# Row length of five of the zero fills in a DMA-bound attention backward kernel: fills 0 and 1 to 56 KB rows, fills 16, 22 and 23 to 28 KB rows

## The chip, the cores and the metric

The kernel runs on one core of a Trainium2 chip. The metric is the device time of one execution in microseconds (us). A profiled execution has a page and a trace; the page's span is about 1.8 us shorter than the time. Each run is labelled fast or slow: slow is a run more than 1.5% above the fastest of the same kernel.

## The reference, cut to what matters

The reference computes a decode step (sliding-window attention over a cache, a small MLP as a gate) and all its gradients. What matters here is the size of the outputs:

```
k_cache, v_cache: (B=2, Hkv=8, Sk=32768, Dh=128) bf16;  window W = 4096
k = k_cache[:, :, Sk - W:, :]      # only the last 4096 of 32768 rows are used
...
return out, d_x, d_k_cache, d_v_cache, d_wq, d_wo, d_w1, d_b1, d_w2, d_b2
```

The gradients of the two caches (out_2, out_3) have the caches' full shape, and their first 28,672 rows per head are zero. So 32 parts (2 caches x 2 batches x 8 heads) of 28,672 x 128 x 2 B = 7.34 MB each must be written with zeros: 235 of the 327 MB that the kernel moves. Each part is one "fill".

## The kernel before

Fills 0 to 30 are issued from GpSimd (POOL), all read the same tile of zero bytes `zt` and cast it to the output's type on the way. The last, 31, is issued from the SP queue at the end.

```python
ZG = 112
zt = const.tile([P, ZG * DH], mybir.dt.uint8, name="zt")
nc.vector.memset(zt[:].bitcast(F32), 0.0)

def zf(o, q, r0, nent, rows, rep=1):        # nent partitions, each writes rep runs of `rows` cache rows
    ...
    w = rows * DH
    if w > ZG * DH:                         # 224 rows: written as f32, so that zt is long enough
        v = v.bitcast(F32); w //= 2
    v = v.rearrange("(r p g) d -> p r (g d)", p=nent, g=rows)
    ...                                     # st: a step of 4 partitions for small pieces, else 1
    zs = zt[0:nent * st:st, 0:w].unsqueeze(1).to_broadcast([nent, rep, w])
    sw_fill.append(nc.gpsimd.dma_start(out=v, in_=zs))

zlong = (3, 5, 7, 11, 12, 16, 17, 18, 19, 22, 23, 24, 25, 26, 27, 28, 29, 30)
zshort = {2: (...), 4: (...), 6: (...), 8: (...), 10: (...), 13: (...), 15: (...), 20: (...)}   # patched fills
for qi in range(ZQ - 1):
    r = 0
    whole = (P, ZR // P, 1) if qi in zlong else (P, ZG, ZR // (P * ZG))   # 56 KB rows, or 28 KB rows twice
    for n, rows, rep in zshort.get(qi, (whole,)):
        r = zf(*zparts[qi], r, n, rows, rep)
```

A "long" fill writes one row of 57,344 B per partition, a "short" one two rows of 28,672 B.

Beside the fills runs the compute chain. It starts with small loads on ACT's queue and large ones on SP's:

```python
dma_store.dma_start(out=b1_bf[:], in_=B_b1.rearrange("(p j) -> p j", j=FK))   # 28 B per partition
dma_store.dma_start(out=b2_bf[:], in_=B_b2.rearrange("(p k) -> p k", k=DK))   # 8 B per partition
dma_load.dma_start(out=w1, ...); dma_load.dma_start(out=w2, ...)
dma_load.dma_start(out=wo[:], ...); dma_load.dma_start(out=wq[:], ...)
vnat = load(A_v_cache, 0, "v")
```

Then come four rounds. Each works on a V tile and a K tile of 4.19 MB, overwrites them with their gradients, stores them (ACT's queue) and loads the next ones into the same buffers. In the last round PE also transposes `oT_all` (line 473), the first step of the output. At the end:

```python
last = nc.sync.dma_start(out=out_6.rearrange("(p k) f -> p k f", k=DK), in_=dw1_st)   # "the dw store"
...                                                     # v, zs: fill 31, 14,336 B rows
with tc.issue_after(last.ins):
    fin = nc.sync.dma_start(out=v, in_=zs)              # also waits for fill 29 (sw_fill[-2])
```

So the dw store marks the end of compute, and fill 31 starts when both the dw store is issued and fill 29 has landed.

## Time and profile before

| | before |
|---|---|
| time, median (4 runs, all fast) | 766.55 us (766.38 to 766.66) |
| DMA rate over the span | 427 GB/s, 326.73 MB |
| PE / DVE / ACT busy | 50% / 36% / 28% |
| first K load issued | 107.3 us |
| dw store issued, fill 31 issued | 701.0 us, 719.1 us |

The first fence is from the page of the kernel before: busy time of each engine (us, share, instructions), the DMA engines' busy tenths and GB/s in 40 equal slices, and the packets, MB and share of each queue. Queue 0 is the fills, 1 is SP's, 10 is ACT's.

```profile
PE 385.0 (50%) x4109; PEld 232.4 (30%) x4118; DVE 275.8 (36%) x483; ACT 214.6 (28%) x313; POOL 35.0 (5%) x67
...
DMA  9999999999999999999999999999999999999998
GB/s 362 426 428 428 436 419 440 435 429 427 426 428 432 430 448 430 413 428 430 438 426 440 430 427 438 425 426 434 437 433 433 433 418 440 431 425 440 430 416 377
...
q0 software_dynamic: 8000, 227.55, 70.4%
q1 hardware_dynamic: 2696, 56.63, 19.2%
q10 hardware_dynamic: 1736, 41.95, 13.6%
```

No compute engine is busy much over half the time, and the DMA engines are at least 90% busy in every slice but the last. The rate is 427 GB/s over the span, and only the first and the last slice fall well below that.

Two lines from the timeline of SP's queue (start us, duration us, what), then the line of SP's waits (total, times, longest) that says what fill 31 waited for:

```profile
107.30 0.54 SPq L217 DMA_DIRECT2D nat<-in_A_k_cache_dram  x1
...
700.97 0.33 SPq L637 DMA_DIRECT2D out_dram<-dw  x1
719.05 0.39 SPq L642 DMA_DIRECT2D out_dram<-zt  x1
```

```profile
SPq L642 <- DMA out_dram<-zt: 17.7, 1, 17.7
```

Fill 31 waited 17.7 us for a fill after compute had ended: compute was not the last to come.

POOL's timeline: after eight issues it waits for fill 0 to land before it may issue more (the bracket is the idle time and what ended it).

```profile
4.92 5.22 POOL L101 DMA_DIRECT2D out_dram<-zt  x8 [3.26 <-DVE zt L81]
43.62 0.60 POOL L101 DMA_DIRECT2D out_dram<-zt  x1 [33.48 <-DMA out_dram<-zt]
```

PE's timeline at line 473. PE stops in mid-group for 7.78 us; "issue" means that the profile shows nothing that it waited for.

```profile
559.96 3.63 PE L408 MATMUL ps<-t,nat 128*128 128x16 bf16 x128
563.52 0.90 PE L473 MATMUL tp<-ident_bf,oT_all 128*2 128x128 bf16 x7
572.20 1.01 PE L473 MATMUL tp<-ident_bf,oT_all 128*2 128x128 bf16 x8 [7.78 <-issue]
```

### The profile page before, as it was taken

The numbers are of one execution on the slowest core, as the hardware profiler recorded it, in microseconds if no ns is written. First come the engines' busy times: TensorE is split into PE (matmuls) and PEld (weight loads), VectorE is DVE, ScalarE is ACT, GpSimd is POOL, SyncE is SP. The second block draws the span as 40 slices with busy tenths as digits, with TensorE's granted clock in tenths as the row PEclk, the third lists the DMA queues.
The fourth block names the chain that finished last, engine by engine and source line by source line (L and its number), as shares of the span: only waits on it lengthen the run. The fifth ranks groups of instructions, "written<-read, shape, count | busy, mean of one in ns | idle before, by whom it ended". The sixth has DMA issues, their size and how long they took to land.

```text
span 764.6 us, 9390 instructions
## 1 busy us (share of the span) xinstructions
PE 385.0 (50%) x4109; PEld 232.4 (30%) x4118; DVE 275.8 (36%) x483; ACT 214.6 (28%) x313; POOL 35.0 (5%) x67
## 2 busy tenths in 40 slices
PE   0166773747503757850665672017539667585000
PEld 0153352533102535420343430015435433231000
DVE  3034252455401447540434652004443526664000
ACT  0034441245500144540113552002323335143000
POOL 3000010010000000000000000000000000000000
PEclk9998898857755886875579686558957657555555
DMA  9999999999999999999999999999999999999998
GB/s 362 426 428 428 436 419 440 435 429 427 426 428 432 430 448 430 413 428 430 438 426 440 430 427 438 425 426 434 437 433 433 433 418 440 431 425 440 430 416 377
DMA packets 12473, 326.73 MB, mean 427 GB/s; under 512 B 2898, under 2 KB 2906, under 8 KB 2934
## 3 DMA queue, kind: packets, MB, share of 16 engines
q0 software_dynamic: 8000, 227.55, 70.4%
q1 hardware_dynamic: 2696, 56.63, 19.2%
q10 hardware_dynamic: 1736, 41.95, 13.6%
q8 instruction: 32, 0.52, 0.3%
q14 instruction: 9, 0.07, 0.0%
HBM read 45.62 MB, written 280.50 MB: 427 GB/s over the span
## 4 chain that ended last, share of the span: by engine, by line
DMA 33%; PE 32%; DVE 11%; ACT 9%; issue 6%; ACTq 0%; DVEq 0%; SPq 0%
DMA out_dram<-nat 14%; DMA nat<-in_A_k_cache_dram 11%; PE ov L419 7%; PE tp L385 5%; DMA b_bf<-in_B_b_dram 4%; DMA nat<-in_A_v_cache_dram 4%; ACT p_bf L453 2%; PE ps L408 2%; ACT nat L157 2%; ACT tring L157 2%; PE s_ps L392 2%; DVE nat L159 2%; PE wps L586 2%; DVE tring L159 2%; PE dops L312 1%
## 5 line engine op out<-in xcount | busy, mean ns | idle before, releaser
L385 PE MATMUL tp<-pperm,nat 128*128 128x128 bf16 x1024 | 91.2, 241 | 142.5 <-DMA nat<-in_A_v_cache_dram 119.3
L159 DVE COPY tring<-tp 128x1024 bf16<-128x1024 bf16 (+1 forms) x98 | 66.0, 689 | 177.4 <-PE tp L385 168.4
L385 PEld LDWEIGHTS <-nat 128*128 128x128 bf16 x1024 | 67.7, 108 | 162.1 <-DMA nat<-in_A_v_cache_dram 121.2
L157 ACT CAST nat<-ov 128x512 bf16<-128x512 f32 x160 | 87.5, 590 | 64.6 <-PE ov L419 42.5
L157 ACT COPY tring<-tp 128x1024 bf16<-128x1024 bf16 (+1 forms) x34 | 34.4, 1011 | 226.1 <-PE tp L385 200.5
L159 DVE CAST nat<-ov 128x512 bf16<-128x512 f32 x96 | 65.6, 690 | 54.7 <-PE ov L419 52.2
L101 POOL DMA_DIRECT2D out_dram<-zt x58 | 33.4, 580 | 529.2 <-DMA out_dram<-zt 525.9
L419 PE MATMUL ov<-bd,ds_bf 128*128 128x512 bf16 x124 | 48.0, 460 | 6.5 <-DVE nat L159 3.7
L419 PE MATMUL ov<-bd,p_bf 128*128 128x512 bf16 x123 | 47.8, 456 | 5.4 <-DVE nat L159 1.4
L408 PE MATMUL ps<-t,nat 128*128 128x16 bf16 x1024 | 28.8, 173 | 14.0 <-issue 7.2
L408 PEld LDWEIGHTS <-nat 128*128 128x128 bf16 x1024 | 28.7, 103 | 16.9 <-issue 11.7
L392 PEld LDWEIGHTS <-zz 128*32 128x32 bf16 x512 | 17.7, 96 | 36.9 <-issue 27.1
L392 PE MATMUL s_ps<-tring,zz 128*32 128x256 bf16 x256 | 19.7, 294 | 14.3 <-ACT tring L157 6.8
L159 DVE CAST wq<-wps 128x512 bf16<-128x512 f32 x16 | 11.0, 691 | 41.3 <-PE wps L579 41.1
L400 PE MATMUL tp<-ident_bf,p_bf 128*128 128x128 bf16 x64 | 7.5, 312 | 34.9 <-ACT p_bf L453 34.9
L392 PE MATMUL dp_ps<-tring,zz 128*32 128x256 bf16 x256 | 20.2, 322 | 7.7 <-ACT tring L157 4.9
L453 ACT ACTIVATE p_bf<-e_sb,rl 32x512 bf16<-32x512 f32 x16 | 22.8, 1424 | 3.4 <-DVE rl L450 3.2
L157 ACT CAST wq<-wps 128x512 bf16<-128x512 f32 x16 | 9.3, 587 | 51.0 <-PE wps L579 51.0
L466 DVE SCALAR_TENSOR_TENSOR ds_bf<-dp_ps,delta,p_bf 32x512 bf16<-32x512 f32 x16 | 21.7, 1357 | 0.3
L419 PEld LDWEIGHTS <-ds_bf 128*128 128x128 bf16 x128 | 13.0, 108 | 20.6 <-issue 18.3
L419 PEld LDWEIGHTS <-p_bf 128*128 128x128 bf16 x128 | 12.9, 110 | 19.9 <-issue 17.3
L400 PEld LDWEIGHTS <-p_bf 128*128 128x128 bf16 x64 | 6.5, 146 | 35.9 <-ACT p_bf L453 35.9
(195 smaller groups left out, 442.4 us busy)
## 6 DMA issues: line engine op xcount, KB each, us to landing
out_dram<-zt POOLq DMA_DIRECT2D x23, 7168.0 KB, 103.3
out_dram<-nat ACTq DMA_DIRECT2D x8, 4096.0 KB, 41.1
out_dram<-zt POOLq DMA_DIRECT2D x7, 3584.0 KB, 64.6
nat<-in_A_v_cache_dram SPq DMA_DIRECT2D x4, 4096.0 KB, 31.5
nat<-in_A_k_cache_dram SPq DMA_DIRECT2D x4, 4096.0 KB, 26.3
out_dram<-zt SPq DMA_DIRECT2D x1, 7168.0 KB, 44.6
out_dram<-zt POOLq DMA_DIRECT2D x2, 3488.0 KB, 67.7
out_dram<-zt POOLq DMA_DIRECT2D x1, 6120.0 KB, 85.8
```

The source lines that it names most:

```text
L101: sw_fill.append(nc.gpsimd.dma_start(out=v, in_=zs))
L157: nc.scalar.copy(out=out_ap, in_=in_ap)
L159: nc.vector.tensor_copy(out=out_ap, in_=in_ap)
L312: nc.tensor.matmul(dops[0:B, :, :], lhsT=dsT_bf[:, dk, :], rhs=woT[:, :, dk, :], start=(dk == 0), stop=(dk == DK - 1))
L385: nc.tensor.transpose(tp[:, j, :], nat[:, g * CC + half * CH + j, :], pperm[:].rearrange("p b k -> p (b k)"))
L392: nc.tensor.matmul(out_ps[pr * RB:(pr + 1) * RB, half * CH * PB:(half + 1) * CH * PB], lhsT=zbuf[:, pr, o:o + RB], rhs=tT[:, :, pr, :], st ...
L400: nc.tensor.transpose(tp[:, cc, :], src[:, half * CH + cc].rearrange("r k b -> r (k b)"), ident_bf[:, :])
L408: nc.tensor.matmul(ps[:], lhsT=nat[:, g * CC + half * CH + cc, :], rhs=cols[half][:, cc, :, g, :], start=(half == 0 and g == 0 and cc == 0 ...
L419: nc.tensor.matmul(ov[:], lhsT=src[:, cc].rearrange("r k b -> r (k b)"), rhs=bd[:, gh * 4:(gh + 1) * 4, :], start=True, stop=True)
L453: nc.scalar.activation(out=p_bf[rb, :, :, pr], in_=e_sb[rb], func=ACT.Copy, scale=rl[rb, 0:1])
L466: nc.vector.scalar_tensor_tensor(out=ds_bf[rb, :, :, pr], in0=dp_c[rb], scalar=delta[rb, 0:1], in1=p_bf[rb, :, :, pr], op0=ALU.subtract, o ...
L586: nc.tensor.matmul(wps[:], lhsT=o_rows[:, j:N:NJ], rhs=ds_rows[:, :], start=True, stop=True)
```

## The change

```diff
-    zlong = (3, 5, 7, 11, 12, 16, 17, 18, 19, 22, 23, 24, 25, 26, 27, 28, 29, 30)
+    zlong = (0, 1, 3, 5, 7, 11, 12, 17, 18, 19, 24, 25, 26, 27, 28, 29, 30)
```

That is all of it. Bytes, order and dependencies stay. The intent can only be in how the fills share the 16 DMA engines with loads and stores: longer rows give the first two fills a larger share, shorter rows give three later fills a smaller one.

## The prediction

> **What bounds the kernel.** The DMA engines. The page's DMA row reads 9 (90% or more busy) in 39 of 40 slices, at 427 GB/s over the span; PE is busy 50%, DVE 36%, ACT 28%. The packet records, in 8 us windows, show 424 to 434 GB/s from 16 to 760 us. 326.7 MB must move, and the change moves the same bytes. The Trainium skill ("DMA: Bandwidth & Descriptors", Specifications) gives 435 GB/s as the fabric ceiling; the trace sits 1 to 2% below it.
>
> **What the change does.** A fill of 7.34 MB goes out as 256 packets of 28,672 B or 128 of 57,344 B. The packet records give 1079 and 2155 ns: per byte 0.1% apart. Windows of fills alone run at 429 to 432 GB/s with long rows, 426 to 431 with short ones. Two fills become long, three short: 128 more packets in queue 0 (8128), same bytes, at most an estimated 0.3 us. POOL's order stays.
>
> **What moves: shares.** The same page (Queues, rings and completion order) says an engine round-robins between queues packet by packet. The trace agrees: against loads of 32,768 B packets, 28 KB fills take about 205 of 430 GB/s (24 to 72 us), 57 KB fills about 271 (464 to 480 us). So:
> - Fills 0 and 1 run at 9.5 to 78 us, beside the loads of w1, w2, wo, wq and the first V, and will take 60 to 80% of the engines instead of half. Fill 0 should land near 34 us (now 43.6, by POOL's waits), fill 1 near 61 (now 77.8), the V tile about 10 us later.
> - The critical chain starts with the bias load b2, 8 B rows, landed at 32.9 us after 8 rounds of about 2.31 us (1079 + 1231). A round with a long packet costs 3.39 us, so I estimate b2 at 40 to 43 us and compute 8 to 10 us later: first K load issued near 116 us instead of 107.3.
> - Fills 16, 22 and 23 run at about 405 to 420 and 545 to 580 us, where the fill queue is alone. Short rows help nobody there, unless the later schedule brings a transfer.
>
> **How much is critical.** Almost nothing: the delay is on the compute chain, which is not the bound. The SP waits show that the last fill, issued on SP at 719.1 us, waited 17.7 us for a fill, not for the store of dw issued at 701.0; compute may be 18 us later before that wait changes. Even then POOL's last fill (done about 745 us) keeps the engines full some 20 us more. Part of the delay should vanish, because a late transfer meets fills that have advanced.
>
> **Prediction:** 766.4 us, 80% range 764.6 to 768.6. Faster by over 2%: 0.01; within 2%: 0.97; slower by over 2%: 0.02.
>
> **What would show it right.** Queue 0 with 8128 packets and 227.55 MB; span mean 426 to 428 GB/s; the first wait in the chain (b_bf) 39 to 41 us instead of 30.9; POOL's first wait for a fill about 10 us shorter; first K load at 113 to 119 us; dw store 0 to 12 us later; last SP fill within 3 us of 719, still released by a fill.
>
> **What would make it wrong.** (a) Delays that add up: transfers that shift from short onto long fills cost about 8 us per 4 MB, and with some 38 us in sum the fills run dry before compute ends. (b) Long packets starving the w1 and w2 loads more than the shares say. (c) Long packets leaving the 16 engines more skewed at the end.

One remark for reading it: its times from packet records were taken on a clock that runs 1.2 us ahead of the page's zero, and so were those in the expectations of meter_early and small_rows below. In the text from here on the two are aligned. And what ran beside the fills in its window of 464 to 480 us were stores, not loads; their packets are of 32,768 B too.

## The result, and the profile after

| | before | after |
|---|---|---|
| time, median of 4 fast runs | 766.55 us (766.38 to 766.66) | 766.27 us (765.98 to 766.32) |
| first K load issued | 107.3 us | 118.2 us |
| dw store issued, fill 31 issued | 701.0 us, 719.1 us | 695.2 us, 725.0 us |
| PE's stop at line 473 | 7.8 us | 2.3 us |

The ratio is 0.9996, with a 95% interval of 0.9978 to 1.0013: the same. A ratio here is the mean time of one kernel's fast runs over that of the other's of the same rounds, so it is not quite the ratio of the medians quoted. The same lines of the page of the kernel after:

```profile
PE 382.6 (50%) x4109; PEld 230.3 (30%) x4118; DVE 275.3 (36%) x483; ACT 214.8 (28%) x313; POOL 35.3 (5%) x67
...
DMA  9999999999999999999999999999999999999998
GB/s 378 412 431 428 439 421 427 445 428 423 426 431 433 432 439 431 418 429 429 436 425 433 440 425 437 427 429 427 430 431 438 430 430 440 427 429 430 429 421 378
...
q0 software_dynamic: 8128, 227.55, 70.3%
q1 hardware_dynamic: 2696, 56.63, 19.9%
q10 hardware_dynamic: 1736, 41.95, 13.8%
```

The 128 more packets are there, with the same bytes and no slice that matters differs. SP's timeline, SP's wait, POOL's timeline and PE's timeline of the kernel after:

```profile
118.18 0.53 SPq L217 DMA_DIRECT2D nat<-in_A_k_cache_dram  x1
...
695.16 0.33 SPq L637 DMA_DIRECT2D out_dram<-dw  x1
724.95 0.39 SPq L642 DMA_DIRECT2D out_dram<-zt  x1
```

```profile
SPq L642 <- DMA out_dram<-zt: 29.4, 1, 29.4
```

```profile
4.92 4.84 POOL L101 DMA_DIRECT2D out_dram<-zt  x8 [3.26 <-DVE zt L81]
35.19 0.60 POOL L101 DMA_DIRECT2D out_dram<-zt  x1 [25.43 <-DMA out_dram<-zt]
```

```profile
559.28 3.64 PE L408 MATMUL ps<-t,nat 128*128 128x16 bf16 x128
562.85 0.91 PE L473 MATMUL tp<-ident_bf,oT_all 128*2 128x128 bf16 x7
566.04 1.12 PE L473 MATMUL tp<-ident_bf,oT_all 128*2 128x128 bf16 x9 [2.28 <-issue]
```

The compute chain moved a good deal and the time did not. Compute is 10.9 us late at the first K load, level at the last K load (507.5 us against 505.8), and 5.8 us early at the dw store. The first shift is the one that was forecast: the wait for the bias load at the head of the critical chain grew from 30.91 to 40.51 us. The last shift was not: the stop of PE at line 473 was 5.5 us shorter. In the packet records, a 16 KB packet of queue 8, which the page calls "instruction", ends 1.3 us before PE goes on (570.9 and 572.2 us), and 1.5 us before in the kernel after (564.6 and 566.0 us); in all fourteen profiles it is 1.3 to 1.6 us. I read this as PE waiting for its next instructions, whose fetch goes through the same 16 DMA engines as the fills; that is a reading of these times, and no run tests it apart from the row length.

The level time thus has two readings. Theory A: bytes bound the time, and everything that happens on the compute chain is hidden. Rival B: the early half of the change costs several us, the late half gains as many, and they cancel. On the stop of PE there is a rival C: its length is chance, and has nothing to do with the row length of the fill that runs beside it.

### The profile page after: what moved, and what is told of

Read it like the earlier page. It is cut to its first block, busy times and chain, and to the rows that moved or that the text cites. A ratio compares the mean times of both kernels' runs of the same rounds, so it can differ in the third digit from the quotient of the medians.

```text
span 764.5 us, 9390 instructions
## 1 busy us (share of the span) xinstructions
PE 382.6 (50%) x4109; PEld 230.3 (30%) x4118; DVE 275.3 (36%) x483; ACT 214.8 (28%) x313; POOL 35.3 (5%) x67
## 3 DMA queue, kind: packets, MB, share of 16 engines
q0 software_dynamic: 8128, 227.55, 70.3%
## 4 chain that ended last, share of the span: by engine, by line
PE 34%; DMA 29%; DVE 13%; ACT 9%; issue 5%; ACTq 0%; DVEq 0%; SPq 0%
DMA nat<-in_A_v_cache_dram 12%; DMA out_dram<-nat 8%; PE tp L385 7%; PE ov L419 6%; DMA b_bf<-in_B_b_dram 5%; DMA nat<-in_A_k_cache_dram 3%; ACT tring L157 3%; ACT p_bf L453 2%; DVE tring L159 2%; ACT nat L157 2%; DVE ds_bf L466 2%; PE s_ps L392 2%; PE wps L586 2%; PE dp_ps L392 2%; PE wps L579 2%
## 5 line engine op out<-in xcount | busy, mean ns | idle before, releaser
L385 PE MATMUL tp<-pperm,nat 128*128 128x128 bf16 x1024 | 88.2, 236 | 133.3 <-DMA nat<-in_A_v_cache_dram 119.2
L385 PEld LDWEIGHTS <-nat 128*128 128x128 bf16 x1024 | 65.3, 105 | 152.9 <-DMA nat<-in_A_v_cache_dram 121.1
L408 PEld LDWEIGHTS <-nat 128*128 128x128 bf16 x1024 | 28.5, 102 | 16.2 <-issue 11.1
L165 PE MATMUL pp<-xT_f,ones_f 128*128 128x2 f32 x8 | 1.9, 356 | 34.7 <-DVE goT L242 34.7
L419 PEld LDWEIGHTS <-p_bf 128*128 128x128 bf16 x128 | 13.1, 111 | 19.8 <-issue 17.1
```

The costliest lines, as they stand in the source:

```text
L385: nc.tensor.transpose(tp[:, j, :], nat[:, g * CC + half * CH + j, :], pperm[:].rearrange("p b k -> p (b k)"))
L408: nc.tensor.matmul(ps[:], lhsT=nat[:, g * CC + half * CH + cc, :], rhs=cols[half][:, cc, :, g, :], start=(half == 0 and g == 0 and cc == 0 ...
L419: nc.tensor.matmul(ov[:], lhsT=src[:, cc].rearrange("r k b -> r (k b)"), rhs=bd[:, gh * 4:(gh + 1) * 4, :], start=True, stop=True)
```

## The experiments

### 1 and 2. Each half of the change alone

early_long has only fills 0 and 1 long in addition; late_short has only fills 16, 22 and 23 short.

```diff
+    zlong = (0, 1, 3, 5, 7, 11, 12, 16, 17, 18, 19, 22, 23, 24, 25, 26, 27, 28, 29, 30)   # early_long
+    zlong = (3, 5, 7, 11, 12, 17, 18, 19, 24, 25, 26, 27, 28, 29, 30)                       # late_short
```

> Only fills 0 and 1 go out as 56 KB rows; 16, 22 and 23 stay long. Theory A (the DMA engines' bytes bound the span, compute is off the critical path): same time, 766.3 us within 0.6 us; b2 lands near 42 us and the first K load is issued near 118 us as after the whole change, and the long instruction wait of PE at the o_rows transposes (line 473), 7.8 us before and 2.3 us after, is again 6 to 9 us because fill 22 is long there, so the store of dw is issued at 700 to 706 us. Rival B (the two halves act on the time and cancel): this half alone is 5 to 10 us slower than before. Rival C (the PE instruction wait was shortened by luck of phase and not by row size): the wait is not tied to this half and may be as short as 2.3 us.

> Only fills 16, 22 and 23 go out as 28 KB rows; 0 and 1 stay short. Theory A: same time, 766.3 us within 0.6 us; first K load at 107 us as before; PE's instruction wait at line 473 near 2.3 us instead of 7.8 us because fill 22 has short rows there, so the store of dw is issued 4 to 7 us earlier than before, at 694 to 697 us, and the last fill some 4 to 6 us later than before. Rival B (halves cancel): 5 to 10 us faster than before. Rival C: the instruction wait is as long as before, 6 to 9 us.

Measured: early_long 766.11 to 766.33 us in five fast runs (ratio 0.9997, 0.9984 to 1.0010), and 791.06 and 793.34 us in two slow ones. late_short 766.27 to 766.45 us in all five (ratio 0.9999, 0.9987 to 1.0011). The kernel before ran 11 times beside them, 766.22 to 766.72 us. So neither half moves the fast runs, and rival B falls.

In late_short the dw store was issued at 691.7 us (2 us earlier than the range expected), fill 31 at 726.0 us (7 us later than before, where 4 to 6 was expected), and the stop at line 473 was 2.5 us. From the list of its waits (total, times, longest):

```profile
PE tp L473 <- issue: 2.5, 1, 2.5
```

In early_long the stop was 8.4 us, as expected; its first K load was issued at 123.3 us (expected near 118), and its dw store missed the expected 700 to 706 us by far. But this profile fell on the 791 us run:

```profile
DMA  9999999999999999999999999999999999998089
GB/s 368 443 411 433 439 423 437 419 442 421 426 426 433 436 436 423 434 426 431 436 429 440 436 415 429 433 438 430 442 431 424 445 421 437 423 426 344 1 375 395
```

```profile
765.43 0.33 SPq L637 DMA_DIRECT2D out_dram<-dw  x1
765.86 0.41 SPq L642 DMA_DIRECT2D out_dram<-zt  x1
```

For 36 of 40 slices the engines ran at the usual rate. Then there was nothing left to move (1 GB/s in the 38th slice): the fills had all landed, compute was not done, and fill 31 was issued only at 765.9 us, just after the dw store. The granted clock does not set the slow runs apart: it was 0.699 and 0.693 in the two, and 0.693 to 0.702 in the five fast runs of small_rows below. This is one look at a slow run, so nothing is concluded from it alone. It asks two questions: how late may compute be, and how much does it vary?

### 3 and 4. Compute made late on purpose

The kernel before, with 10 or 30 in-place copies that depend on the last evacuation (the copy of PE's last result into the tile that is stored) and that the dw store depends on:

```diff
             evac(dw1_st[:, k, n0:n0 + n], wps[:, 0:n])
+    dwf = dw[:, 0:DK * F].bitcast(F32)
+    for _ in range(10):        # store_late_30: range(30)
+        nc.vector.tensor_copy(out=dwf, in_=dwf)
```

> The kernel before, with ten in-place copies of dw (3584 f32 per partition) on VectorE between the last evacuation and the store of dw; each takes an estimated 1.9 to 3.8 us from the 3.05 us fill of 3584 f32 zeros in the trace, so the store is issued some 19 to 38 us late, at 720 to 739 us. Theory A: the fill queue keeps the engines full until 745 us, so the time stays at 766.4 us within 1 us. Rival B or any reading in which compute bounds the kernel: later by nearly the whole delay.

> As store_late_10 with thirty copies: store of dw issued 57 to 114 us late, at T = 758 to 815 us. Theory A: the fills run dry about 743 us, and from then on the time is the issue of the dw store plus its 1.84 MB and the last fill's 7.34 MB at 430 GB/s (21.3 us) plus about 2 us, so about T + 23 us; the delay costs only what goes beyond some 40 us. Compute-bound reading: the whole delay is added to the time.

Measured: store_late_10 766.20 to 766.47 us with the dw store at 726.75 us, ratio 0.9999 (0.9986 to 1.0012). SP's timeline:

```profile
726.75 0.33 SPq L640 DMA_DIRECT2D out_dram<-dw  x1
```

Compute that ended some 26 us later cost nothing. store_late_30 787.24 to 796.25 us, ratio 1.0329 (1.0298 to 1.0360). Its profile (796.25 us): the added line's instructions (min/median/max ns, first and last start us), then the page, then SP's timeline:

```profile
L620 DVE COPY dw<-dw x30: 2026/2027/2028, 708.8 to 768.6; 128x3584 f32<-128x3584 f32 x30
```

```profile
DMA  9999999999999999999999999999999999999219
GB/s 356 437 422 428 441 419 448 417 434 427 425 436 431 426 448 415 430 429 427 433 439 434 431 428 421 435 428 445 434 432 428 422 433 432 432 430 438 116 69 393
```

```profile
770.65 0.33 SPq L640 DMA_DIRECT2D out_dram<-dw  x1
771.08 0.39 SPq L645 DMA_DIRECT2D out_dram<-zt  x1
```

The time is the dw store's issue plus 796.25 - 770.65 = 25.6 us. Of this, 21.3 us are the 9.18 MB of the dw store and fill 31 at 430 GB/s. So I take the time as the larger of 766.3 us and T + 25.6 us, where T is the issue of the dw store; compute is free as long as T is below an estimated 766.3 - 25.6 = 740.7 us. The slow early_long run fits without being used for it: 765.43 + 25.6 = 791.03 us, measured 791.06. So do the four metered profiles below, with T from 753.7 to 811.4 us and 25.6 us from the dw store to the end in each. Between 728.2 us, the latest T that a profile shows to be free, and 753.7 us nothing was measured.

A second use of this kernel: since the fills always run dry in it, its time shows in every run, profiled or not, when compute ended. The four runs differ by 9 us. As the copies come after everything else, I take this spread to be in the kernel before too, where it is hidden.

### 5 to 8. A meter for the end of compute

The thirty copies in the kernel after, in each half, and in the kernel with fills 0 and 1 long and 16 short, but 22 and 23 long.

```diff
+    zlong = (0, 1, 3, 5, 7, 11, 12, 17, 18, 19, 24, 25, 26, 27, 28, 29, 30)                  # meter_after
+    zlong = (0, 1, 3, 5, 7, 11, 12, 16, 17, 18, 19, 22, 23, 24, 25, 26, 27, 28, 29, 30)      # meter_early
+    zlong = (3, 5, 7, 11, 12, 17, 18, 19, 24, 25, 26, 27, 28, 29, 30)                        # meter_late
+    zlong = (0, 1, 3, 5, 7, 11, 12, 17, 18, 19, 22, 23, 24, 25, 26, 27, 28, 29, 30)          # meter_early_16
+    for _ in range(30):
+        nc.vector.tensor_copy(out=dwf, in_=dwf)
```

> The kernel after, with the thirty copies of store_late_30, so that every run's time shows when compute ended (time = issue of the dw store + about 24 us, in the runs of store_late_30 787 to 796 us with a median of 791.6). If the change as a whole makes compute end earlier, as its profile shows (695.2 instead of 701.0 us), the median is 784 to 788 us and the spread no wider than with the rows of before. If the two profiles differ only by the run-to-run spread, the median is within 2 us of 791.6.

> early_long with the thirty copies. The profile of early_long's 791 us run had its K loads on long fills (156.2 instead of 143.2 us for the first, 431.7 instead of 394.3 us for the third) and its dw store at 765.4 us. Theory D (delays add up when transfers slip onto long fills, and fill 16 long is one such place): times are later and wider than meter_after, median 795 to 815 us, some runs 845 to 865 us. Rival (the two slow runs were the chip's own slow state and not the kernel's schedule): 786 to 796 us in fast runs, as narrow as the others.

> late_short with the thirty copies. Its profile had the dw store at 691.7 us against 701.0 before, mostly from the shorter instruction wait of PE: median 780 to 786 us, 6 to 10 us below store_late_30. If row size of fills 16, 22 and 23 has no effect on compute (rival: luck of phase): 789 to 794 us.

> Fills 0 and 1 long, 16 short, 22 and 23 long, with the thirty copies. If fill 16 is what keeps late transfers from slipping onto long rows, the spread is as narrow as meter_after and no run is beyond 805 us, with a median 5 to 8 us above meter_after because the instruction wait of 7 to 9 us under fill 22 is back. If fills 22 and 23 are what keeps the kernel from the slow runs, it is as wide as meter_early.

| metered kernel | every run, us (beyond 1.5% of its fastest, so labelled slow: in brackets) |
|---|---|
| before (store_late_30) | 787.2, 791.3, 791.9, 796.3 |
| late half | 784.3, 784.5, 785.3, 787.2 |
| the whole change | 779.3, 780.9, 787.6, (792.7), (815.1), (847.7) |
| early half | 785.5, 785.8, 796.1, (798.3), (854.5), (874.8) |
| early half with fill 16 short | 789.4, 796.9, 798.1, (835.4), (836.9), (837.7) |

In these kernels the label only says that compute ended late, so all runs are shown. The late half is 6.7 us below before by the medians (784.89 and 791.59), as expected; PE's stop is 4.2 us shorter in its profile (3.2 and 7.4 us), which is most of that and not all. The early half's median of 797.2 us and its latest runs are near what was expected. The whole change has the earliest runs of all and also very late ones. My expectation of a median of 784 to 788 us for it, no wider than before, was wrong (790.14 us): I had taken one profile for the kernel. What widens the spread is the early half: all three kernels that have it are wide (48 to 89 us), and the two without it are not (3 and 9 us). That fill 16 keeps it narrow was wrong too: meter_early_16 has three of six runs beyond 835 us. With six runs each it stays open what fill 16 and what fills 22 and 23 contribute to the spread.

The copies move the dw store by 61.9 us (SP's wait for them is 68.2 us, where it was 6.3 us), so a metered time of M stands for a dw store at M - 61.9 - 25.6 = M - 87.5 us without them. The limit of 740.7 us is M = 828 us; I had worked with 84 and 826. By that, one of the six runs of the whole change would have passed it, two of the six of the early half, three of the six with fill 16 short, and none of before or of the late half.

### 9. The kernel after again

> The kernel after, unchanged. A metered time M stands for an unmetered dw store at about M - 84 us (779.3 for the profile with 695.2), and the fills run dry when that store is later than about 742 us, which is M above 826: one of the six meter_after runs (847.7). So fast runs at 766.3 us within 0.4 us, and of about seven runs none or one or two beyond 770 us, none over 800 us. Rival (the slow runs of early_long have nothing to do with the schedule): the kernel before shows as many slow runs as this one in the same rounds.

Measured: 765.85, 766.05, 766.24, 766.47 and 766.82 us, and one run of 802.92 us, where none over 800 us was expected. Ratio of the fast runs 0.9997 (0.9985 to 1.0010). None of the 37 runs of the kernel before is above 767.21 us; of the ten of the kernel after one is. The slow run has no profile. The rule just found would ask for a dw store at 777 us there, beyond what the meter showed (at most 847.7 - 87.5 = 760 us), so this run's cause is inferred, not shown, and the size is larger than I expected.

The profile is of the 765.85 us run, the fastest of either kernel. SP's timeline, PE's stop from the list of waits, and the page:

```profile
120.92 0.54 SPq L217 DMA_DIRECT2D nat<-in_A_k_cache_dram  x1
...
728.23 0.33 SPq L637 DMA_DIRECT2D out_dram<-dw  x1
728.65 0.41 SPq L642 DMA_DIRECT2D out_dram<-zt  x1
```

```profile
PE tp L473 <- issue: 8.0, 1, 8.0
```

```profile
DMA  9999999999999999999999999999999999999998
GB/s 375 416 438 421 447 417 442 428 426 426 431 430 430 431 443 429 419 437 423 431 429 439 437 430 419 429 434 431 431 430 442 430 428 430 433 428 438 417 429 382
```

The same kernel, in two fast runs: the dw store at 695.2 us in one and at 728.2 us in the other, and the times 766.32 and 765.85 us. This is the plainest proof that compute is off the critical path. PE's stop was 8.0 us here and 2.3 us in the first profile: compute came some 28 us later to line 473 and met fills 24 and 25, which are long, instead of 22 and 23, which are short. So the stop follows the row length of the fill that happens to be there, in one and the same kernel. The two profiles also show how delays grow. From the packet records of both:

| first K load | issued | last packet | packets moving for | fill bytes moved meanwhile in 57 KB packets |
|---|---|---|---|---|
| after, first profile | 118.2 us | 142.0 us | 17.3 us | 1.9 of 3.2 MB |
| after, second profile | 120.9 us | 154.3 us | 26.9 us | 6.5 of 7.4 MB |

A load issued 2.7 us later landed 12.3 us later, because it met almost only fill 5, which has long rows, where the other had also met the end of fill 4, which has short ones. That is how the early delay can add up instead of vanishing. And fill 16 does act where a late chain reaches it: the third K load met it in both kernels, moving for 20.0 us with 0.2 of 4.3 MB of fill in long packets in this profile (fill 16 short), and 31.1 us with 9.2 of 9.2 MB in long ones in that of early_long (fill 16 long).

### 10. Smaller rows everywhere

The kernel before with 14 KB rows in all whole fills, and 7 KB rows in fills 0 and 1.

```diff
-        whole = (P, ZR // P, 1) if qi in zlong else (P, ZG, ZR // (P * ZG))
+        g = 28 if qi < 2 else 56
+        whole = (P, g, ZR // (P * g))
```

> All whole fills in 14 KB rows (fills 0 and 1 in 7 KB rows), the eight patched fills as they are. Theory of five packets: a transfer or an instruction fetch that joins a busy engine waits for about five fill packets that the engine has already taken, plus about 2.5 us (13.1 us behind 57,344 B packets, 7.8 us behind 28,672 B ones); so behind 14,336 B packets of about 0.54 us the first packet of the last V store comes 4.5 to 6 us after its issue, and PE's instruction wait at line 473 (7.8 us, 2.3 us) is under 1 us. Loads and stores get about 70% of the engines, compute ends earlier, dw store at 630 to 680 us. The time is still 766.3 us within 1 us, because bytes bound it. Rival (row size sets the DMA rate): slower by 1 to 3% with smaller rows. Compute-bound reading: 20 us or more faster.

Measured: 767.56 to 767.71 us in five runs, ratio 1.0014 (1.0002 to 1.0026): the same by the 2% rule, and 0.3 us outside the expected 766.3 us within 1 us. The rival's 1 to 3% falls. Queue line of the page, SP's timeline and SP's wait:

```profile
q0 software_dynamic: 17216, 227.55, 71.8%
```

```profile
99.66 0.53 SPq L218 DMA_DIRECT2D nat<-in_A_k_cache_dram  x1
...
646.48 0.33 SPq L638 DMA_DIRECT2D out_dram<-dw  x1
730.89 0.39 SPq L643 DMA_DIRECT2D out_dram<-zt  x1
```

```profile
SPq L643 <- DMA out_dram<-zt: 84.0, 1, 84.0
```

Compute ended 54.5 us before that of the kernel before, and the kernel was 1.05 us slower by the medians. If the packets are the cost, 1.05 us x 16 engines / 9216 more packets is an estimated 1.8 ns a packet; that cause was not separated from others. For the 128 packets of the change the same estimate is 0.015 us.

The stop at line 473 by row length of the fill beside it, over all profiles:

| rows of the fill beside it | PE's stop at line 473, us |
|---|---|
| 57,344 B (8 profiles) | 7.4, 7.7, 7.8, 8.0, 8.4, 8.4, 8.4, 8.9 |
| 28,672 B (4 profiles) | 2.3, 2.5, 2.5, 3.2 |
| mostly 28,160 B, of a patched fill (2 profiles) | 2.2, 2.9 |

The long and the short group do not touch, so rival C falls: beside long rows this stop is about 5 us longer.

The traces hold a second test. PE makes two more such stops later, at lines 537 and 408, also 1.2 to 1.6 us after the end of a 16 KB packet of queue 8. In all twelve profiles with long rows there they last 4.9 to 6.8 us and 6.0 to 7.2 us. In the two with 14,336 B rows, PE does not stop at line 537 at all; at line 408 it does not stop in one, and in the other it stops at the same instruction as elsewhere, the 94th of 128, for 0.45 us. No profile has 28,672 B rows there.

But my picture of a fixed number of five packets ahead of a newcomer is wrong. For PE's stop it asked for less than 1 us. Lines 537 and 408 meet that; line 473 did not test it cleanly, because at that moment a patched fill with 28,160 B rows was being taken up. The better test is the first packet of the last V store, on an idle queue behind 14 KB rows: 6.6 us after its issue (7.8 us on the clock of the expectation), where 4.5 to 6 was expected. Behind rows of 28 KB and a little less, first packets of stores on an idle queue took 6.4 to 6.8 us, behind long rows alone 10.8 to 12.4 us. For these stores, rows beyond 28 KB lengthen the wait and rows below it do not shorten it; what sets that floor stays open, and so does why PE's later stops all but vanish there.

### 11. Fills that start earlier

small_rows with the zero tile set in two pieces:

```diff
-    nc.vector.memset(zt[:].bitcast(F32), 0.0)
+    nc.vector.memset(zt[:, 0:28 * DH].bitcast(F32), 0.0)
+    nc.vector.memset(zt[:, 28 * DH:].bitcast(F32), 0.0)
```

> As small_rows, with the zero tile set in two pieces, the first quarter of it first, so that fills 0 and 1 can be issued some 2 us earlier than 4.9 us. Only time in which the engines are not full can be gained: before the fills start the loads alone move 210 to 340 GB/s, so about 2 us times 100 to 200 GB/s, 0.2 to 0.45 MB, 0.5 to 1.0 us less than small_rows: 765.3 to 765.8 us. If the start is bounded by something else, no gain.

Measured: 767.62 to 767.71 us, no gain over small_rows (767.56 to 767.71). The first fill packet did start earlier, at 6.6 instead of 9.9 us, and the span did not shrink. This expectation was wrong, and the packet records show why: by 10 us both kernels had moved the same 2.96 MB, of which 0.47 MB were fill here and almost nothing in small_rows. The loads alone had moved 396 to 438 GB/s from 4 to 8 us in small_rows, not 210 to 340, so the earlier fill only took the place of loads.

### 12. One fill less

The kernel before without fill 17: 7.34 MB of out_3 stay unwritten.

```diff
     for qi in range(ZQ - 1):
+        if qi == 17:
+            continue
```

> The kernel before without fill 17 (wrong on purpose: one of 32 zeroed parts of 7.34 MB stays unwritten). If bytes bound the time, it is shorter by 7.34 MB at 430 GB/s = 17.1 us, 749.3 us within 1.5 us, as long as compute (dw store 701 us) still ends before the fills run dry (725 us). If compute bounds it, the gain is less than 3 us.

Measured: 749.23 to 749.58 us, median 749.34 us, ratio 0.9775 (0.9763 to 0.9788), with the outputs wrong. The gain, 766.58 - 749.34 = 17.24 us, is 7.34 MB at 426 GB/s, though compute ended at 710.3 us, later than in the profile before. So bytes bound the time.

## Why the prediction was right or wrong

**The bound and the time: right.** 766.27 us against a forecast of 766.4 us. Bytes bound the time (one_less), 33 us of compute more or less change nothing (the two profiles of after), and store_late_30 gives the limit: the dw store may be issued up to about 740.7 us. I had written that delays of some 38 us in sum are free; from 701.0 us the measured room is 39.7 us.

**The cost of the packets: right.** 8128 packets and 227.55 MB in queue 0, 427 GB/s.

**The shares at the start: right, sizes near.** The Trainium skill ("DMA: Bandwidth & Descriptors", Queues, rings and completion order) has the engines take turns between queues by packet, and the trace agrees: fill 0 let POOL go on at 35.2 us (forecast about 34, before 43.6) and fill 1 at 63.3 us (forecast about 61), the bias load's wait was 40.51 us (forecast 39 to 41), the first K load was issued at 118.2 us (forecast 113 to 119). The V tile landed 7.5 us later in the packet records (forecast about 10).

**"Short rows help nobody there": wrong.** This was said of fills 16, 22 and 23, because no load or store ran beside them. One transfer did, as I read queue 8: the fetch of PE's own instructions. Short rows cut PE's stop at line 473 from 7.4 to 8.9 us to 2.3 to 3.2 us. I had looked for transfers that the kernel issues and had overlooked queue 8, though the page before lists it: 32 packets, 0.52 MB. Hence two further misses: "dw store 0 to 12 us later" (it was 5.8 us earlier in the first profile), and "last SP fill within 3 us of 719" (725.0 us). The second follows from the first: loads and stores that come earlier take DMA time ahead of fill 29. In the packet records fill 29 ends 5 us later, and 2.4 MB more of other transfers, 5.5 us at 427 GB/s, have been moved by then. That compute ended early in the first profile was partly luck: in the second the same kernel met a long fill at line 473, and its dw store came 27 us later than before, not 0 to 12.

**"Part of the delay should vanish": half right.** It vanished in the first profile and grew in the second. The prediction named growth as its first way to be wrong, with a chance of 2% that the kernel is over 2% slower. One of ten runs was (802.92 us). As a statement on single runs 2% looks too low, though one in ten runs does not settle it.

**No version beats both.** The two kernels and the two halves tie at 766.3 us in fast runs. The late half alone has the earliest steady end of compute (784.3 to 787.2 us metered, four runs) without the early half's spread.

## What to carry to other kernels

When, as here, the DMA engines are full from end to end and a deep queue of independent transfers is behind them, row lengths mostly decide who waits (over the lengths tried here the time of fast runs moved by 0.14% at most); price a change by its bytes first, and then ask how much room the compute chain has before that queue runs dry. Measure that room instead of arguing it: a dependent delay before the last store gives the limit, and the same delayed kernel shows the hidden spread of compute in every timed run, which a single profile does not. Look at the instruction queue too among the transfers that a long DMA row may hold up.

## What the Trainium skill lacked or had wrong

- "Runtime: NRT & Kernel Launch", Instruction fetch mechanics, has instructions fetched by DMA in blocks of 16 KiB and calls the cost of a block mostly hidden; it gives no cost for DMA engines that are full. Here 16 KB packets marked "instruction" in queue 8 shared the engines with the fills, and PE stood still at line 473 for 7.4 to 8.9 us beside 57,344 B rows, and for 2.2 to 3.2 us beside rows of 28,672 B and less.
- "DMA: Bandwidth & Descriptors", SWDGE vs HWDGE vs iDMA, prefers packets of at most 4096 B as the switching unit. The trace records one packet for each whole row here, 57,344 B in 2155 ns and 28,672 B in 1079 ns, and the queues' shares follow these.
- The same page, Latency and other measured facts, gives about 600 ns to the first byte of a DMA from SP or ACT. At the start, before the fills, SP's first load had its first packet 1.0 us after the issue. On full engines and an idle queue of ACT the first packet came 6.4 to 12.4 us after the issue, the more where 57,344 B rows were ahead.
- The same page, Bandwidth, says that the HBM side at about 358 GB/s binds transfers between HBM and SBUF, though it also has 425 GB/s for one core with its neighbour idle. The one core of this program held 427 GB/s over 765 us, 281 of 327 MB being writes, which fits the second figure and not the first; what the neighbour did is not on record.
